# First-weight blocks of a joint matrix product: split by the loader or ahead of the store

## The chip, the cores and the metric

One core of one Trainium2 chip. The metric is the time of one execution on the device in microseconds (us), as the median of several runs. Engines are named as in the profile: PE (TensorE matmuls), PEld (its weight loads), DVE (VectorE), ACT (ScalarE), POOL (GpSimd), SP (SyncE, which mostly issues DMAs). "SPq" is SP's own queue of instructions.

## The reference

Attention within chunks of 64 positions, followed by a mixer of rank 32 along the sequence and a two-layer network with relu:

```python
B, H, S, D = 8, 8, 576, 64          # chunk = 64, so 9 chunks per head
scores = scale * q_c @ k_c.T        # in each chunk of 64
attn = exp(scores - max(scores));  attn = attn / sum(attn)
x = (attn @ v_c)                    # put back to [8, 576, 512]
xt = x.transpose(0, 2, 1)
h = xt @ U @ V                      # U [576, 32], V [32, 576]
u = x + h.transpose(0, 2, 1)
ch = maximum(u @ w_ch1, 0.0) @ w_ch2    # 512 -> 2048 -> 512
return u + ch
```

All inputs and the output are float32. On the chip a float32 operand of the big products is split into a high part rounded to fp32r and a low part (value minus high part), and a product of two operands is made of three: high by high, high by low, low by high.

## The kernel before, in words

The eight batches form four pairs `pr`. A pair has nine tiles of 128 positions by 512 channels (in three groups of three). In time the kernel has these parts, by the profiled run:

- **0 to 150 us, lead.** The weights are brought in and split into high and low parts (the areas `area[f]`, sixteen of them, one for each 128 of the 2048 hidden channels, with both weight matrices of that block), and pair 0 goes through attention. A planner sets the order.
- **150 to about 416 us, blocks.** Seven groups of three tiles go through the two layers block by block: `hidden` (L1070), relu and split (L1078 on ACT, L1083 on DVE), `project_out` (L1098). Between the blocks stand the "visits", which do the attention of a later pair (scores L894, softmax L907 to L921, values L949, the turn of the exponentials through HBM as `exs` and `eT`, split of x L974 on ACT and L978 on DVE or POOL, the product with U L991/L992) and the "mixes", which add V's part and put the mixed rows to HBM (`xd`, `xb`, `ud`, `xs`, `uf`).
- **416 us to the end, `joint`.** The remaining eight groups go two at a time through four rounds (`JOINT`), each of 4 chunks. Here the first layer is not computed block by block but with Strassen's scheme in Winograd's form: seven products of sums of weights with sums of activations instead of eight. In a chunk there are fourteen such product steps (A1 to A7 and B1 to B7, named in `STEPS`; six matmuls each, L1495) and twelve output steps (Ga0 to Gb5, L1471). After certain steps ACT copies a bank (`snap`, L1426), DVE adds to a bank (L1429, L1441), and ACT and DVE make the relu and its split (L1437, L1438). The sums of activations for the next round are made by POOL (`csum`, L1365 to L1371) and split by ACT (L1391) and DVE (L1392).

Each product step needs one block of (sums of) first weights, 256 by 256 numbers. These are made once, in `combos(i)` for i = 0 to 7: POOL builds the sums (L1285 to L1290), `parts` splits them on ACT (L1296) and on the side chosen by `queues` (L1297) and puts them to HBM as `wc[i]`, `plain_parts` puts the three unsummed blocks there from the areas, where high and low part lie already (L1309, L1310). They come back as a stream of 224 blocks (4 rounds x 4 chunks x 14 steps) of high and low part together, 256 KB each: `issue(n)` loads block n to `window(n)`, one of `LOADS = 11` places; the load of block n + 11 is issued right after product n. To make room for these places and for the sums of activations, `gather(i)` copies the second weights of every odd area into the even one before it, HBM not being involved.

What sets the order: after the lead, everything but the blocks hangs in an agenda by ticks (`at(tick, name, run)`); three or four ticks are a block, one tick is one step of `joint`. A table `TUNE["shift"]` adds to the tick of each named piece (as `"wpart 0": 4`), and `TUNE["queues"]` says on which queue its DMA is issued (S, P, A for SP, POOL, ACT) or, for the subtractions of splits (`xl`, `clo`, `wlo`), whether POOL ("P") or DVE makes them. Instructions of one engine run in the order in which they are written; a DMA whose data or place is not ready holds up everything behind it on the queue that issues it. `dma(kind, ...)` (L217) issues nearly all DMAs, so that line 217 stands for all kinds, and the tile names tell them apart.

Of the kernel before, what the change touches and what calls it, by code (L numbers as in the profile page):

```python
# [1669 lines left out]
```

## Time and profile before

| | |
|---|---|
| three runs | 1020.01, 1016.02, 1019.69 us; median 1019.69 us |
| the profiled execution | 1021.43 us, of which the span from first to last instruction is 1019.6 us |
| mean granted clock of PE | 0.956 of full speed |
| PE, DVE, ACT, POOL busy | 90%, 58%, 29%, 21% of the span |
| mean busy share of the 16 DMA engines | high (0.8 to 0.97) from 225 to 750 us, 0.48 after that |

How to read it: PE is the engine with most work, so the time is PE's work at full clock plus what PE stands idle plus what a lower granted clock adds. A view by stretches of time gives for each stretch each engine's busy time, the granted clock (PEclk, 1.0 is full speed) and the busy share of the DMA engines; a view of waits gives what ended each of PE's idle times; the chain of waits follows the end of the run back to what released each step.

### The profile page before, as it was taken

Reading aid. Unit: us, or ns where it says so; the run is one execution under the profiler, and the core shown is the slowest. Engines: PE = TensorE matmul, PEld = TensorE weight load, DVE = VectorE, ACT = ScalarE, POOL = GpSimd, SP = SyncE. Lnnn points to the kernel's source line nnn. Section 1 sums busy time; section 2 is a strip of 40 time slices with the busy share of each in tenths; the row PEclk is TensorE's granted clock in tenths of the full one; section 3 lists DMA queues with packets and bytes.
Section 4 is the critical chain, followed back from the end, with each engine's and each line's share of the span. In section 5 each row is a group of like instructions: output and inputs, shape, how many; then the busy total and the mean of one; then the engine's idle time right before and its main releaser. Section 6 shows DMA issues by size and latency. Waiting matters only on the chain.

```text
span 1019.6 us, 17395 instructions
## 1 busy us (share of the span) xinstructions
PE 917.1 (90%) x6404; PEld 796.1 (78%) x6404; DVE 592.5 (58%) x1134; ACT 300.8 (29%) x600; POOL 213.0 (21%) x318
## 2 busy tenths in 40 slices
PE   6899999988868868989589899897989999999998
PEld 5579988876757757969477797886978998799987
DVE  4899975674645544855567745555553545644333
ACT  5576731222212112412031521222331322222211
POOL 4200002376824111402022601102320011200000
PEclk9999999999879978989699999988999999999999
DMA  9975756678789998999699887938745667364311
GB/s 181 225 265 146 198 125 147 145 217 207 207 252 290 262 251 249 285 253 236 179 232 225 263 255 204 251 105 226 225 145 175 207 193 231 108 212 145 124 52 63
DMA packets 329796, 202.94 MB, mean 199 GB/s; under 512 B 202480, under 2 KB 276240, under 8 KB 329712
## 3 DMA queue, kind: packets, MB, share of 16 engines
q1 hardware_dynamic: 215904, 168.25, 56.9%
q10 hardware_dynamic: 106320, 15.37, 9.1%
q0 software_dynamic: 7488, 18.21, 6.4%
q8 instruction: 51, 0.84, 0.3%
q14 instruction: 33, 0.27, 0.1%
HBM read 145.93 MB, written 65.80 MB: 208 GB/s over the span
## 4 chain that ended last, share of the span: by engine, by line
PE 49%; DMA 10%; DVE 5%; SPq 4%; issue 1%; ACT 1%; ACTq 0%; DVEq 0%
PE o L1471 23%; SPq L217 4%; PE o L1098 3%; DMA eT<-exs 3%; DMA w<-wc 3%; PE h L1070 3%; PE x_0B L1495 2%; PE x_1A L1495 2%; PE x_0A L1495 1%; PE x_2A L1495 1%; PE x_1B L1495 1%; DVE w L1392 1%; PE x_3A L1495 1%; PE x_3B L1495 1%; PE as L949 1%
## 5 line engine op out<-in xcount | busy, mean ns | idle before, releaser
L1070 PE MATMUL h<-uth,w 128*128 128x384 f32 x512 | 144.9, 349 | 7.9 <-DVE x L961 7.9
L1479 DVE TENSOR_TENSOR xr<-o,xr 128x512 f32<-128x512 f32 x96 | 65.5, 687 | 112.2 <-PE o L1471 102.2
L1098 PE MATMUL o<-w,hh 128*128 128x512 f32 x384 | 124.2, 405 | 2.2 <-ACT hh L1078 2.2
L217 POOL DMA_DIRECT2D vn<-in_v_dram x104 | 63.9, 625 | 221.0 <-PE as L894 136.8
L1070 PEld LDWEIGHTS h<-uth,w 128*128 128x128 f32 x512 | 98.0, 196 | 11.5 <-issue 9.3
L1070 PE MATMUL h<-utl,w 128*128 128x384 f32 x256 | 89.3, 349 | 0.0
L1098 PEld LDWEIGHTS o<-w,hh 128*128 128x128 f32 x384 | 72.6, 193 | 15.7 <-ACT hh L1078 3.5
L1098 PE MATMUL o<-w,hl 128*128 128x512 f32 x192 | 78.2, 407 | 1.9 <-DVE hl L1083 1.9
L1078 ACT ACTIVATE hh<-h 128x384 fp32r<-128x384 f32 x64 | 31.0, 488 | 124.8 <-PE h L1070 120.6
L1083 DVE SCALAR_TENSOR_TENSOR hl<-h,hh 128x384 fp32r<-128x384 f32 x64 | 34.9, 548 | 38.1 <-ACT hh L1078 37.9
L949 PE MATMUL as<-vn,eT 64*64 64x64 f32 x864 | 26.4, 252 | 32.2 <-DMA eT<-exs 21.9
L914 ACT ACTIVATE ex<-ex 128x512 f32<-128x512 f32 x27 | 17.1, 632 | 127.8 <-DVE ex L908 105.7
L1070 PEld LDWEIGHTS h<-utl,w 128*128 128x128 f32 x256 | 50.2, 196 | 2.6 <-issue 0.2
L949 PEld LDWEIGHTS as<-vn,eT 64*64 64x64 f32 x864 | 22.1, 161 | 35.8 <-issue 23.6
L1098 PEld LDWEIGHTS o<-w,hl 128*128 128x128 f32 x192 | 36.9, 192 | 13.9 <-DVE hl L1083 5.5
L217 POOL DMA_DIRECT2D xb<-xd x22 | 12.2, 556 | 135.3 <-DMA xd<-x 30.8
L907 DVE TENSOR_REDUCE mx<-as 128x4 f32<-128x256 f32 x54 | 22.5, 416 | 27.8 <-PE as L949 26.2
L874 DVE STREAM_TRANSPOSE qn<-qn 128x512 f32<-128x512 f32 x27 | 19.0, 704 | 31.1 <-DMA qn<-qblocks 28.8
L1471 PE MATMUL o<-w,hh_3B 128*128 128x512 f32 x96 | 32.5, 422 | 0.0
L1471 PE MATMUL o<-w,hh_0A 128*128 128x512 f32 x96 | 31.8, 414 | 0.0
L1471 PE MATMUL o<-w,hh_1A 128*128 128x512 f32 x96 | 31.5, 410 | 0.0
L1471 PE MATMUL o<-w,hh_1B 128*128 128x512 f32 x96 | 31.5, 410 | 0.0
(338 smaller groups left out, 2092.9 us busy)
## 6 DMA issues: line engine op xcount, KB each, us to landing
w<-wc SPq DMA_DIRECT2D x220, 256.0 KB, 3.7
wraw<-in_moe_w_ch_dram SPq DMA_DIRECT2D x32, 512.0 KB, 5.8
xs<-xb SPq DMA_DIRECT2D x112, 64.0 KB, 3.2
uf<-xs SPq DMA_DIRECT2D x27, 256.0 KB, 4.6
vn<-in_v_dram POOLq DMA_DIRECT2D x104, 64.0 KB, 4.2
kblocks<-in_k_dram ACTq DMA_DIRECT2D x23, 288.0 KB, 6.0
qblocks<-in_q_dram ACTq DMA_DIRECT2D x22, 288.0 KB, 6.1
exs<-ex SPq DMA_DIRECT2D x96, 64.0 KB, 3.2
```

The lines of the kernel that those rows point to most:

```text
L217: {"S": nc.sync, "P": nc.gpsimd, "A": nc.scalar}[way].dma_start(dst, src)
L874: nc.vector.transpose(z, z)
L907: nc.vector.reduce_max(mx[:, e], self.sc[e].rearrange("p (h k) -> p h k", k=C), axis=AX.X)
L914: nc.scalar.activation(exf, exf, AF.Exp, scale=SCALE)
L949: nc.tensor.matmul(ps[e][cs, (HP + hp) * C : (HP + hp + 1) * C], lhsT=self.eT[rows, hp, 2 * c : 2 * c + 2, :].rearrange("p a i -> p (a i)" ...
L1070: nc.tensor.matmul(ps[:, :GN], lhsT=w[:, z, cc], rhs=u[:, cc, :], start=(n == 0), stop=(n == 3 * NCC - 1))
L1078: nc.scalar.activation(hh, ps[:, :GN], AF.Relu)
L1083: nc.vector.scalar_tensor_tensor(hl, ps[:, :GN], 0.0, hh, op0=ALU.max, op1=ALU.subtract)
L1098: nc.tensor.matmul(acc[j], lhsT=h[:, js], rhs=w2[f][:, z], start=(first and i == 0), stop=(final and i == 2),)
L1471: nc.tensor.matmul(acc[j], lhsT=u[:, q, js], rhs=w2[f][:, p], start=(z == "A" and e == 0 and n == 0), stop=(z == "B" and e == 1 and n == 2),)
L1479: nc.vector.tensor_add(xs[j], acc[j], xs[j])
L1495: nc.tensor.matmul(ps, lhsT=w[:, wz ^ low_first, cc], rhs=u[uz][:, cc], start=(k in (1, 2, 5) and cc == 0 and m == 0), stop=(cc == 1 and m ...
```

## The change

The stream holds single float32 blocks instead of high and low parts. `combos(i)` makes the sums as before on POOL, but in four regions of the two spare tiles, and `put()` stores all seven blocks of an i, the plain ones among them (POOL's first two additions make high plus low, which is the plain float32 weight), in four DMAs of kind `wput`. `parts`, `plain_parts` and `gather` are gone, and with the last the moved second weights: `window(n)` is now a pair of half-size places, one in the first weights' part of an even area and one in that of the odd one, and a load brings 128 KB into the low place. New is `split_w(n)`: ACT rounds the block from the low place into the high place (L1321 of the new kernel), then POOL (or DVE for four of the 224, by `queues`) subtracts in place so that the low part stays (L1322). It stands in the program behind product n - 5 (`AHEAD = 5`), the first five at ticks of their own (`wsplit`). The first loads are due five ticks earlier (+9 for +14). Both tables of `TUNE` are replaced as a whole; among other things the fetches of `xb` go from POOL's queue to SP's, and most exceptions for single transfers are gone. Lines behind the tables stand 16 to 18 lower than before.

Counted in the two programs: SP issues 868 DMAs instead of 830; ACT has 859 instructions instead of 652, POOL 489 instead of 318, DVE 1126 instead of 1134; PE has 5238 in both.

```diff
-        "wsum 4": 2.5, "wsum 5": -2.75, "wsum 6": -6, "wsum 7": 5
...
+        "wsplit 1": -4, "wsplit 2": -1.75, "wsplit 3": -2, "wsplit 4": 0.25, "wsum 0": 4.0,
...
-        "clo 3.0.5": "S", "clo 3.1.3": "S", "clo 3.2.4": "P", "fetch": "P", "fetch 1_1": "S",
...
+    QUEUES = {"vn": "P", "perm": "A", "wlo": "P", **TUNE.get("queues", {})}
...
     LOADS = 11
+    AHEAD = 5
...
         def sums():
             done.add(("sum", i))
-            assert i < 2 or ("parts", i - 2) in done
-            wc[i] = dram.tile([7, P, 2, KC], F32, name=f"wc_{i}")
-            st["b"] = rooms()
...
+            assert not i or ("put", i - 1) in done
+            one, two, r1, r2 = st["b"] = [region(k) for k in range(4)]
...
-        def parts():
-            done.add(("parts", i))
-            for t, k in zip(st["b"], (3, 5)):
-                h, b = t[:, DM : 2 * DM], t[:, i % 2 * 2 * DM :][:, 0:DM]
-                nc.scalar.copy(h, b.bitcast(F32))
-                side("wlo", i).tensor_sub(b, b.bitcast(F32), h)
-                nc.sync.dma_start(
...
+        def put():
+            done.add(("put", i))
+            if not i % 2:
+                wc[i // 2] = dram.tile([P, len(ORDER), KC], F32, name=f"wc_{i // 2}")
+            to = wc[i // 2]
+            one, two, r1, r2 = st["b"]
+            for src, ks in ((one, (1, 2)), (two[:, KC:], (3,)), (r1, (5, 4)), (r2, (6, 7))):
...
-    def plain_parts(i):
...
-        nc.sync.dma_start(wc[i][0:2].rearrange("k p z x -> p z k x"), one)
-        nc.sync.dma_start(wc[i][2], two[:, :, 1])
...
-    def gather(i):
...
-        dma("gather", even[:, 0 : 2 * DM].bitcast(F32), odd[:, 2 * DM :].bitcast(F32))
...
     def window(n):
         k = n % LOADS
         if k < 7:
-            return whole[2 * k + 1][:, 6 * KC : 8 * KC]
-        return whole[NF - 1][:, (k - 7) * 2 * KC : (k - 6) * 2 * KC]
+            return [area[2 * k + z][:, 3 * KC :] for z in range(2)]
+        k -= 7
+        a = area[2 * 7 + k // 2][:, (k % 2) * 2 * KC : (k % 2 + 1) * 2 * KC]
+        return [a[:, 0:KC], a[:, KC:]]
...
-        dma("w", window(n).bitcast(F32), wc[i][KEPT[k]].rearrange("p z x -> p (z x)"), n)
+        dma("w", window(n)[1].bitcast(F32), wc[c][:, o], n)
+
+    def split_w(n):
+        if n >= BLOCKS_OF * len(JOINT):
+            return
+        assert ("issue", n) in done
+        done.add(("wsplit", n))
+        h, l = window(n)
+        nc.scalar.copy(h, l.bitcast(F32))
+        side("wlo", n).tensor_sub(l, l.bitcast(F32), h)
...
                     issue(n + LOADS)
+                    split_w(n + AHEAD)
...
-        at(f"wpart {i}", FIRST + 6 * i + 5, parts)
-        at(f"wplain {i}", 182 + 5 * i, lambda i=i: plain_parts(i))
-        at(f"gather {i}", 192 + 8 * i + 4, lambda i=i: gather(i))
+        at(f"wput {i}", FIRST + 6 * i + 5, parts)
...
-        at(f"first {n}", 192 + 8 * n + 14, lambda n=n: issue(n))
+        at(f"first {n}", 192 + 8 * n + 9, lambda n=n: issue(n))
+        if n < AHEAD:
+            at(f"wsplit {n}", 192 + 8 * n + 16, lambda n=n: split_w(n))
```

How the instructions of three engines stand now. A row names the line, the operation, the tile written, the tile read, and its shape; the number at the end of a name is the tile's own; "x4" is four like it in a row.

SP in the part from 300 to 415 us, before; `w<-w` of 1024 columns is a gather, `wc<-w` a plain part, `w<-wc` the first loaded block, `exs` and `eT` the turn of the exponentials, `qn` and `kn` the loads of a visit:

```order
L217 DMA w_614<-w_951 128x1024
L217 DMA qn_2_3503<-qblocks_2435 128x4x128
L217 DMA kn_2_3504<-kblocks_2436 128x4x128
L217 DMA qn_3_3580<-qblocks_2435 128x4x128
L217 DMA kn_3_3581<-kblocks_2436 128x4x128
L217 DMA exs_0_3593<-ex_0_3486 32x4x128 x4
L217 DMA xd_8_3605<-x_8_3493 128x512
L217 DMA eT_0_3607<-exs_0_3593 128x4x32 x4
L217 DMA w_951<-wc_2379 128x512
L1309 DMA wc_2746<-w_1396 256x2x256
L1310 DMA wc_2746<-w_1454 256x1x256
L217 DMA eT_1_3623<-exs_1_3616 128x4x32 x4
```

The same engine and place now, where `xb<-xd` is a fetch:

```order
L201 DMA qn_2_3480<-qblocks_2439 128x4x128
L201 DMA kn_2_3481<-kblocks_2440 128x4x128
L201 DMA w_951<-wc_2393 128x256
L201 DMA exs_0_3526<-ex_0_3454 32x4x128 x4
L201 DMA exs_1_3540<-ex_1_3464 32x4x128 x4
L201 DMA xb_6_3545<-xd_6_3197 128x512
L201 DMA qn_3_3572<-qblocks_2439 128x4x128
L201 DMA kn_3_3573<-kblocks_2440 128x4x128
L201 DMA xb_4_3581<-xd_4_2857 128x512
L201 DMA xb_5_3592<-xd_5_2864 128x512
L201 DMA eT_1_3611<-exs_1_3540 128x4x32 x4
L201 DMA w_1082<-wc_2393 128x256
```

Gathers and plain parts are gone from the row, the loads of blocks are half as wide, and the fetches stand in it.

ACT in chunk 1 of the last round, before; L1426 is a copy of a bank, L1437 a relu:

```order
L1426 COPY s_3_1A<-x_1A 128x384
L1426 COPY s_3_1A<-c_1A 128x384
L1426 COPY u_3_1A<-x_1A 128x384
L1437 ACTIVATE hh_1A<-y_1A 128x384
L1437 ACTIVATE hh_1A<-c_1A 128x384
L1426 COPY s_3_1B<-x_1B 128x384
L1426 COPY u_3_1A<-x_1A 128x384
```

The same engine and place now; L1408 is the copy, L1419 the relu, L1321 the rounding of a loaded block:

```order
L1408 COPY s_3_1A<-x_1A 128x384
L1321 CAST w_1021<-w_1082 128x256
L1408 COPY s_3_1A<-c_1A 128x384
L1321 CAST w_1128<-w_1160 128x256
L1321 CAST w_1219<-w_1259 128x256
L1408 COPY u_3_1A<-x_1A 128x384
L1419 ACTIVATE hh_1A<-y_1A 128x384
L1321 CAST w_1306<-w_1353 128x256
L1321 CAST w_1396<-w_1454 128x256
L1419 ACTIVATE hh_1A<-c_1A 128x384
L1408 COPY s_3_1B<-x_1B 128x384
L1321 CAST w_1500<-w_1550 128x256
```

One rounding per product step has come between the copies and relus.

POOL in the first round, before; `vn` are loads of v for a visit, `xb` fetches:

```order
L217 DMA vn_4_4452<-in_v_dram 64x4x64 x4
L217 DMA vn_5_4489<-in_v_dram 64x4x64 x4
L217 DMA xb_2_4746<-xd_2_4232 128x512
L217 DMA xb_1_4775<-xd_1_4049 128x512
L217 DMA xb_3_4835<-xd_3_4257 128x512
L217 DMA vn_7_4939<-in_v_dram 64x4x64 x4
L217 DMA vn_6_4979<-in_v_dram 64x4x64 x4
L217 DMA vn_8_5186<-in_v_dram 64x4x64 x4
```

The same engine and place now; L1322 is the subtraction that leaves the low part:

```order
L1322 TENSOR_TENSOR w_1454<-w_1454,w_1396 128x256
L201 DMA ud_1_4943<-xb_1_4819 128x512
L1322 TENSOR_TENSOR w_1550<-w_1550,w_1500 128x256
L1322 TENSOR_TENSOR w_1607<-w_1607 128x256 x2
L1322 TENSOR_TENSOR w_1649<-w_1649 128x256
L201 DMA vn_7_5024<-in_v_dram 64x4x64 x4
L1322 TENSOR_TENSOR w_1649<-w_1649 128x256
L201 DMA vn_8_5227<-in_v_dram 64x4x64 x4
L201 DMA vn_1_5243<-in_v_dram 64x4x64 x4
L1322 TENSOR_TENSOR w_1082<-w_1082,w_1021 128x256
```

Subtractions stand on POOL's queue in front of and behind the loads of v.

## Rows read from the trace of the kernel before

**Rows 1.** The page's line of busy time, share of the span and instructions.

```profile
PE 917.1 (90%) x6404; PEld 796.1 (78%) x6404; DVE 592.5 (58%) x1134; ACT 300.8 (29%) x600; POOL 213.0 (21%) x318
```

**Rows 2.** Stretches: length, busy PE, PEld, DVE, ACT, POOL, PEclk, DMA share, GB/s.

```profile
225.00:300.00 75.00, 56.13 (x432) 47.96 (x433) 44.22 (x79) 14.72 (x27) 48.60 (x60) 0.85 0.84 219
300.00:415.00 115.00, 96.44 (x759) 83.67 (x758) 61.29 (x128) 24.05 (x51) 28.42 (x42) 0.92 0.97 266
415.00:750.00 335.00, 293.27 (x2076) 255.00 (x2076) 202.22 (x413) 89.13 (x204) 69.94 (x106) 0.93 0.81 220
750.00:1019.60 269.60, 263.52 (x1323) 234.85 (x1322) 115.14 (x200) 66.34 (x151) 18.35 (x27) 0.99 0.48 153
```

**Rows 3.** PE's waits, 225 to 300 us: total us, times, longest.

```profile
PE as L949 <- DVE hl L1083: 7.3, 1, 7.3
```

**Rows 4.** PE's waits, 300 to 415 us.

```profile
PE y L991 <- ACT xh L974: 9.3, 1, 9.3
```

**Rows 5.** PE's waits, 415 to 750 us.

```profile
PE as L949 <- DMA eT<-exs: 16.8, 13, 3.5
```

**Rows 6.** The chain of waits, 340 to 396 us: start, duration, what.

```profile
362.82 4.07 DMA xs<-xb
```

**Rows 7.** The chain of waits, 474 to 500 us.

```profile
477.39 7.96 DMA w<-wc
```

**Rows 8.** DMA, 300 to 415 us: totals; issues with count, KB, median us to landing.

```profile
DMA packets 51035, 30.62 MB, mean 266 GB/s; under 512 B 28958, under 2 KB 45345, under 8 KB 51025
...
wc<-w SPq DMA_DIRECT2D x8, 512.0 KB, 5.4
w<-w SPq DMA_DIRECT2D x8, 512.0 KB, 4.8
wc<-w SPq DMA_DIRECT2D x8, 256.0 KB, 5.4
w<-wc SPq DMA_DIRECT2D x8, 256.0 KB, 3.7
```

**Rows 9.** DMA, 415 to 750 us, the same view.

```profile
DMA packets 116776, 73.79 MB, mean 220 GB/s; under 512 B 69187, under 2 KB 92739, under 8 KB 116748
...
w<-wc SPq DMA_DIRECT2D x113, 256.0 KB, 4.3
...
eT<-exs SPq DMA_DIRECT2D x48, 64.0 KB, 3.7
```

**Rows 10.** Groups by line and form: count, busy us, mean ns, idle before, releaser.

```profile
L1391 ACT CAST w<-us 128x256 fp32r<-128x256 f32 x48 | 17.4, 404 | 7.3 <-POOL us L1369 2.8 <-POOL us L1371 2.3 <-POOL us L1365 1.9
L1371 POOL TENSOR_TENSOR us<-uf,uf 128x256 f32<-128x256 f32 x12 | 9.7, 820 | 6.7 <-DVE w L1392 6.7
L217 POOL DMA_DIRECT2D vn<-in_v_dram x104 | 63.9, 625 | 221.0 <-PE as L894 136.8 <-DVE qn L874 20.0 <-PE as L949 19.4
L1297 DVE TENSOR_TENSOR wch<-wch 128x512 fp32r<-128x512 f32 x8 | 9.9, 1237 | 14.4 <-ACT wch L1296 14.4
L978 DVE TENSOR_TENSOR xl<-x,xh 128x512 fp32r<-128x512 f32 x23 | 15.5, 683 | 14.9 <-ACT xh L974 11.5 <-DMA xs<-xb 2.1 <-DMA exs<-ex 1.1
```

**Rows 11.** The waits of SP's own queue, 225 to 300 us.

```profile
SPq L1298 <- DVE wcl L1297: 8.4, 1, 8.4
```

**Rows 12.** Timeline, 927 to 931 us: start, duration, engine, line, instruction.

```profile
928.70 1.20 PE L1495 MATMUL c_1B<-w,w 128*128 128x384 f32 x6
928.95 0.48 ACT L1426 COPY u_1A<-x_1A 128x384 f32<-128x384 f32 x1 [0.35 <-PE x_1A L1495]
...
929.74 1.20 PE L1495 MATMUL x_1A<-w,w 128*128 128x384 f32 x6
```

**Rows 13.** POOL's waits, 415 to 750 us.

```profile
POOL us L1365 <- DMA uf<-xs: 30.2, 4, 18.5
...
POOL vn L217 <- DVE qn L874: 20.0, 1, 20.0
POOL vn L217 <- PE as L949: 19.4, 2, 18.8
```

More of the change, by code (lines that the diff above doesn't have):

```diff
@@ L1266, in combos, with region @@
         st = {}
[L1268 to L1269 removed]
+        def region(k):
+            if not turned_w:
                 for z in "hl":
[L1271 removed]
+                    turned_w[z] = work.tile([P, NCC, GN], F32, tag="ut" + z, name="wc" + z, bufs=2).rearrange(
                         "p c t -> p (c t)"
                     )
[L1274 to L1275 removed]
+            z, k = divmod((4 * i + k) % 6, 3)
+            return turned_w["hl"[z]][:, k * DM : (k + 1) * DM]
         def sums():
             done.add(("sum", i))
[L1279 to L1282 removed]
+            assert not i or ("put", i - 1) in done
+            one, two, r1, r2 = st["b"] = [region(k) for k in range(4)]
             for b, f in ((one, 2 * i), (two, 2 * i + 1)):
@@ L1303, in combos @@
-        return sums, parts
-    def plain_parts(i):
-        assert ("gather", i) not in done
-        done.add(("plain", i))
-        one, two = (area[f].bitcast(F32).rearrange("p (z k x) -> p z k x", z=2, k=2) for f in (2 * i, 2 * i + 1))
-        nc.sync.dma_start(wc[i][0:2].rearrange("k p z x -> p z k x"), one)
-        nc.sync.dma_start(wc[i][2], two[:, :, 1])
-    stream = [
-        (2 * c + "AB".index(z[0]), int(z[1])) for _ in JOINT for c in range(CHUNKS) for z in STEPS if z[0] != "G"
-    ]
@@ L1316, in gather @@
-    def gather(i):
-        assert ("plain", i) in done and ("sum", i) in done and ("hidden", 1, 0, 2 * i) in done
-        done.add(("gather", i))
-        even, odd = (whole[f] for f in (2 * i, 2 * i + 1))
-        dma("gather", even[:, 0 : 2 * DM].bitcast(F32), odd[:, 2 * DM :].bitcast(F32))
-        moved[2 * i + 1] = even[:, 0 : 2 * DM].rearrange("p (s x) -> p s x", s=2)
-    moved = {}
+            nc.gpsimd.tensor_sub(r1[:, a], two[:, a], one[:, a])
+            nc.gpsimd.tensor_sub(r2[:, z], two[:, z], two[:, a])
@@ new lines, in sums @@
+            nc.gpsimd.tensor_sub(r2[:, a], two[:, z], r1[:, a])
+            nc.gpsimd.tensor_sub(r1[:, z], one[:, z], r2[:, a])
+        def put():
[5 more added lines that the diff above has]
+            for src, ks in ((one, (1, 2)), (two[:, KC:], (3,)), (r1, (5, 4)), (r2, (6, 7))):
+                at = [ORDER.index("AB"[i % 2] + str(k)) for k in ks]
+                dma(
+                    "wput",
+                    to[:, at[0] : at[-1] + 1 : max(1, at[-1] - at[0])],
+                    src.rearrange("p (k x) -> p k x", x=KC),
+                    i,
+                )
@@ L1325, in window @@
+        return sums, put
+    ORDER = [z for z in STEPS if z[0] != "G"]
+    BLOCKS_OF = len(ORDER) * CHUNKS
     def window(n):
@@ L1384, in split @@
             done.add(("split", self.s, j, k))
-            assert ("gather", i) in done and ("out", 1, 0, 2 * i + 1) in done
+            assert free(2 * i + 1)
             assert not self.s or ("last", self.s - 1, k) in done
@@ L1487, in joint @@
                     loads[0] += 1
-                    w = window(n).rearrange("p (z c f) -> p z c f", z=2, c=2)
-                    low_first = KEPT[k] > 2 and not (2 * c + "AB".index(z)) % 2
+                    w = [v.rearrange("p (c f) -> p c f", c=2) for v in window(n)]
                     u = combo(k)
@@ L1496, in joint @@
                                 ps,
-                                lhsT=w[:, wz ^ low_first, cc],
+                                lhsT=w[wz][:, cc],
                                 rhs=u[uz][:, cc],
@@ L1502, in joint @@
                             )
-                    assert ("issue", n) in done and all(("split", s, i, k) in done for i in range(GT))
+                    assert ("wsplit", n) in done and all(("split", s, i, k) in done for i in range(GT))
                     done.add(("product", n))
@@ L1632 @@
             pend = (pr, g, f, hs)
-    w2.update({f: moved[f] for f in range(1, NF, 2)})
     for n in range(7, LOADS):
```

27 lines of the change are left out of this document (7 added, 20 removed), and 253 rows, old and new, of the table TUNE.

## The prediction

> **What bounds the kernel now.** I read the page's busy line first: PE works 917.1 us of a span of 1019.6 [rows 1], so about 102 us are to be had at most without touching its work, plus what a lower clock adds. The second view, the stretches, tells where. For each I add PE's idle time and the part of its busy time that the clock below 1.0 costs, (1 - PEclk) times busy [rows 2]: 225 to 300 us loses 18.9 + 8.4 = 27.3; 300 to 415 loses 18.6 + 7.7 = 26.3; 415 to 750 loses 41.7 + 20.5 = 62.2; 750 to the end only 6.1 + 2.6 = 8.7. The third view, PE's waits, tells on what: between 225 and 300 us the longest ends with DVE's split of the relu [rows 3]; between 300 and 415 with ACT's rounding of a visit's x [rows 4], whose data come through HBM; between 415 and 750 the waits for the turned exponentials `eT` lead with 16.8 us in 13 waits [rows 5]. No row names a block of first weights as what PE waited for, so the stream itself is early enough. The last view, the chain, shows how it acts all the same: it passes through transfers that took long when the DMA engines were full, a 64 KB `xs` of 4.07 us [rows 6], and once through a block load of 7.96 us [rows 7], against which the median load of the stretch lands in 4.3 us [rows 9]; from that landing the chain goes on with SP's own next issues, so that what was queued behind it on SP started late. In the stretches from 225 to 750 us the DMA engines are 0.81 to 0.97 busy, behind 750 us 0.48 [rows 2]. So fewer bytes and fewer issues can buy time only before 750 us, and there they act on waits that other transfers end.
>
> **The parts of the change.** The sum is made on the profiled run, 1021.4 us, which is its span and 1.8 us around it; the median of the runs is 1.7 lower.
>
> *1. Gathers and plain parts gone (300 to 415 us).* Removed from this stretch are 8 gathers and 8 plain parts of 512 KB and 8 plain parts of 256 KB, 8 x 1280 KB = 10.5 MB, and half of 8 loads of 256 KB, 1.0 MB: 11.5 of 30.62 MB, or 38% [rows 8]. 24 issues leave SP's queue. DMA is the fullest resource here (0.97), and what PE loses is mostly late data, so I let the loss shrink in proportion: 38% of 26.3 = **-10.0**. Bounds: 0, if the waits are latency and not load, and -26.3, if all of it goes.
>
> *2. Loads of half the size (415 to 750 us).* 113 loads lose 128 KB each, 14.8 of 73.79 MB, 20% [rows 9]. In proportion: 20% of 62.2 = **-12.4**. Bounds: 0, and -41.7, the whole idle time. Behind 750 us as many loads shrink too, but PE is idle for 6.1 us there: nothing.
>
> *3. Split of the sums gone (225 to 300 us).* Sixteen subtractions leave DVE, the eight of one half alone 9.9 us [rows 10], and as many roundings leave ACT. SP waited 8.4 us for one of these subtractions before it could store its result [rows 11]; it now waits for POOL's sums alone, which are unchanged. The stores are as large as before within a fifth (8 x 896 KB for 16 x 512 KB). Of the 7.3 us that PE waits for DVE's relu split [rows 3], behind which those subtractions stood in part, I take about half: **-4**. Bounds: 0 and -18.9, the idle time of the stretch.
>
> *4. Rounding and splitting each block.* No such instruction is in the trace, but ACT rounds the same shape in 404 ns and POOL subtracts it in about 820 ns [rows 10]: 224 x 0.404 = 90 us more on ACT, 220 x 0.82 = 180 us more on POOL. Both have the room on average: ACT goes from 301 to about 380 us (ten of them back from part 3), POOL from 213 to about 393. What counts is where they stand. In a joint round product steps follow each other by 1.04 us (928.70 to 929.74). ACT's copy of a bank starts 928.95 and takes 0.48, so the bank is free at 929.43, and PE's next product in that bank begins at 929.74: a margin of 0.31 us [rows 12]. A rounding put right before such a copy begins earlier than the copy could (ACT was idle for 0.35 us there), so that it is covered in most places; uncovered it would cost 0.404 - 0.31 = 0.09 us for each of 128 copies, 12 us. At the three ends of rounds, where ACT also rounds the next sums in a row, two roundings more stand between the copies after B6 and B7: 3 x 2 x 0.404 = **+2.4**. On POOL a subtraction has a cover of four to five products, since its block is needed five products later: 5 x 1.04 - 0.40 - 0.82 = 4.0 us. Bounds: 0 and 12 + 2.4 = +14.4.
>
> *5. The order.* PE's own order is nearly the same; visits move by a step or so. The 22 fetches of `xb` go from POOL's queue to SP's, behind which `exs`, `eT` and the block loads wait if a fetch waits for its data. What a new order gives or takes is not in any row; I bound it by the longest single waits of the two stretches, 7.3 and 9.3 us [rows 3, 4], as about 8 us either way, and take **0**, since the transfers that were moved to SP replace 24 that left it.
>
> Sum: -10.0 - 12.4 - 4 + 2.4 = -24.0, so 1021.4 - 24.0 = 997.4 on the profiled run; 1.7 less for the median: **about 995.5 us**, rounded to 995.
>
> **The rivals.**
>
> *A. The relief does not reach PE: about 1020.* The stream is halved but the waits stay. For it: a 64 KB `eT` lands in 3.7 us, a 256 KB block in 4.3 [rows 9], so that size matters little once a transfer is alone, and PE's largest sum of waits is on `eT` [rows 5]. Against it: the `xs` of 4.07 and the load of 7.96 us [rows 6, 7] are long for their size, which is load. Parts 1 to 3 at nothing and +2.4 for part 4 make 1023.8 on the profile; a little relief in part 1 alone makes it 1020 on the median. The Trainium skill, "DMA: Bandwidth & Descriptors", section "Anatomy of one DMA — SWDGE (gpsimd) path", speaks for this rival: it fits a transfer as some 2.0 us fixed plus bytes over 436e3, by which an estimate for a load is 2.6 us at 256 KB and 2.3 at 128 KB. By it part 2 would be worth 0.3 us on a load that PE does not wait for, nothing in the sum. The page speaks of transfers that GpSimd issues and these are SP's; the median landing of 4.3 us is 1.7 us longer than the estimate, which is what the trace says of queueing.
>
> *B. POOL's queue becomes the bound (slower): about 1037.* POOL works in order. Loads of v wait in its queue until PE has freed their place, and sums for the next round wait for their data: between 415 and 750 us 30.2, 20.0 and 19.4 us in seven waits [rows 13]. If subtractions stand behind these, the weights of the next products come late, and PE stops in the middle of a round. Each wait has 4.0 us of cover: 69.6 - 7 x 4.0 = 41.6 us, which on 997.4 makes 1039.0, or 1037 on the median. It makes the kernel slower from about 24 us on. For it: subtractions do stand right behind the loads `vn_7`, `vn_8` and `vn_1` in the new order, and one wait lasts 18.8 us. Against it: those waits belong to loads issued early; the new table moves most of the loads of v, and what waited with nothing behind it can be put where it waits for nothing.
>
> *C. The clock comes back as well: about 974.* PE's clock is at 0.92 and 0.93 in the stretches in which it pauses and 0.99 where it doesn't [rows 2]. If the pauses get short enough for the full clock, 7.7 + 20.5 = 28.2 us of clock loss go from 300 to 750 us, and idle time goes in proportion, 38% of 18.6 and 20% of 41.7, 15.4. With -4 and +2.4 the sum is -45.2: 976.2, or 974 on the median. Against it: visits, which cause the pauses by their chain through HBM, all stay.
>
> *D. POOL and DVE slow each other: about 1010.* DVE's subtraction of two tiles took 1237 ns while POOL made the sums of the weights, and the same shape 683 ns in the visits [rows 10]. With 220 more subtractions on POOL the same 0.55 us may come on DVE's two-input splits. On the path are those at the three ends of rounds, three tiles times three late sums: 27 x 0.55 = 14.9 us, 1012.3 or 1010 on the median. A rule of the Trainium skill speaks for this: "SBUF — State Buffer", section "Who interferes with whom", has one port pair shared by the two engines under an exclusive lock, and a DVE instruction with two SBUF inputs contends with a GpSimd one that reads SBUF. The two rows agree with it, but they don't show which of the two engines was first.
>
> **How the numbers follow.** Forecast 995: 0.43. Rival B 0.18, as the only new serial queue; C 0.15; A 0.14; D 0.10. A measurement of this kernel can tell about 0.5%, 5 us, from no change. Faster by more: the forecast, C, nearly all of D and a little of A, 0.43 + 0.15 + 0.09 + 0.02 = 0.69. Within: most of A, the edges of B and D, 0.10 + 0.01 + 0.01 = 0.12. Slower: B and the rest of A, 0.17 + 0.02 = 0.19. The range goes from somewhat below C, 968, to 1030: this takes in A, D and the half of B in which only some of its seven waits reach PE, and leaves out about 0.09 above and as much below, where all bounds of parts 1 to 3 are met.
>
> **What would show it.** Part 1: in the stretch from 300 to 415 us, which should end about 10 us earlier, the DMA share falls from 0.97 and the wait on `xh` shrinks. Part 2: the loads land sooner than 4.3 us and the sum of `eT` waits falls below 16.8 us. Part 3: SP no longer waits there for DVE, and the wait for L1083 is about half. Part 4: PE's waits on ACT's copies in the last 270 us stay within some 3 us of 6.1 us idle; ACT is near 380 and POOL near 393 us busy. B would show as PE waiting at the product steps for POOL's L1322; D as DVE's splits of sums rising from their present means; C as a clock of 0.97 or more from 415 to 750 us. The forecast is wrong if the stretches before 750 us keep their lengths, or if the stretch behind it, now full, gets longer.

## The result, and the profile after

The changed kernel takes 987.5 us in the median of three runs (986.96 to 987.66), against 1019.69 before: a ratio of 0.9694, 95% interval 0.9659 to 0.9728, or 32 us less. 995 had been forecast, so the sign and the order of size are right, and the gain was larger than the 24.7 us forecast.

The busy line and the stretches of the changed kernel (columns as in [rows 2], the last stretch being shorter by what was won):

```profile
PE 907.8 (92%) x6404; PEld 788.2 (80%) x6404; DVE 590.7 (60%) x1126; ACT 360.0 (37%) x808; POOL 346.7 (35%) x489
```

```profile
225.00:300.00 75.00, 59.03 (x456) 49.53 (x455) 38.38 (x81) 12.21 (x24) 40.45 (x51) 0.90 0.89 225
300.00:415.00 115.00, 103.99 (x828) 90.90 (x826) 69.38 (x148) 33.40 (x82) 40.33 (x59) 0.99 0.76 190
415.00:750.00 335.00, 304.60 (x2164) 265.07 (x2165) 209.46 (x404) 123.86 (x315) 143.03 (x195) 0.95 0.68 177
750.00:985.90 235.90, 229.63 (x1127) 204.67 (x1125) 107.25 (x181) 86.18 (x227) 79.60 (x104) 0.99 0.32 96
```

PE is idle for 11.0 us between 300 and 415 us where it was 18.6, its granted clock there is 0.99 for 0.92, and the DMA engines are 0.76 busy for 0.97 [rows 2]. From 415 to 750 us idle time falls from 41.7 to 30.4 us, DMA from 0.81 to 0.68. The last stretch keeps its 6 us. DMA from 300 to 415 us and from 415 to 750 us:

```profile
DMA packets 46905, 21.90 MB, mean 190 GB/s; under 512 B 30751, under 2 KB 42184, under 8 KB 46894
...
w<-wc SPq DMA_DIRECT2D x18, 128.0 KB, 3.9
```

```profile
DMA packets 118879, 59.30 MB, mean 177 GB/s; under 512 B 70052, under 2 KB 108565, under 8 KB 118847
...
w<-wc SPq DMA_DIRECT2D x116, 128.0 KB, 3.3
eT<-exs SPq DMA_DIRECT2D x56, 64.0 KB, 3.2
```

Against [rows 8, 9] a block lands in 3.3 us instead of 4.3 in the second stretch, and `eT` in 3.2 instead of 3.7; in the first a block of half the size lands no sooner (3.9 us for 3.7). PE's waits of 225 to 300 us and of 415 to 750 us (total, times, longest), and SP's own of 225 to 300 us:

```profile
PE y L975 <- ACT xh L958: 8.2, 1, 8.2
PE as L933 <- DMA eT<-exs: 3.1, 5, 1.3
```

```profile
PE as L933 <- DMA eT<-exs: 10.9, 13, 4.0
PE x_0B L1476 <- ACT u_0B L1408: 5.9, 2, 4.3
PE x_3B L1476 <- ACT u_3B L1408: 3.7, 2, 2.4
PE x_2A L1476 <- ACT u_2A L1408: 3.0, 1, 3.0
PE as L878 <- DVE kn L858: 2.9, 1, 2.9
PE x_1B L1476 <- ACT u_1B L1408: 2.2, 2, 1.1
PE c_3B L1476 <- POOL w L1322: 1.4, 1, 1.4
```

```profile
SPq L201 <- POOL wch L1273: 2.5, 1, 2.5
```

The wait for the relu split [rows 3] is gone; SP's wait of 8.4 us for a subtraction of the sums [rows 11] has become one of 2.5 us for POOL's sums and two shorter ones. The wait of 9.3 us for `xh` [rows 4], before the eleventh of the visits' products with U, is gone; before the ninth, of an earlier visit, there is now one of 8.2 us. In the joint rounds PE now waits longest for ACT's copies of banks (L1408), and once for a split block (L1322). Waits for copies are not new, however: from the start of round 1 on they are 14.8 us in the kernel before and 18.3 now, while those for `eT` fall from 16.8 to 10.9. Their largest row before, from 417 us on:

```profile
PE x_3B L1495 <- ACT u_3B L1426: 8.4, 3, 3.8
```

Fixed stretches of time mix different work, so for the rest I cut each run at places of the program: the start of the first matmul of every eighth block of hidden units, and of each joint round, from the trace; round 4 goes to the end of PE's last matmul. Ahead of the joint rounds stand four groups of three tiles (not seven, as the description of the kernel has it), of sixteen such blocks each, so that blocks 32 to 63 are the last two groups. Us in each part, in one profiled execution of each kernel:

| kernel | start of block 32 | blocks 32-39 | 40-47 | 48-55 | 56-63 | round 1 | round 2 | round 3 | round 4 |
|---|---|---|---|---|---|---|---|---|---|
| before | 200.8 | 57.2 | 56.7 | 56.3 | 45.8 | 179.7 | 161.1 | 132.3 | 126.3 |
| changed | 202.5 | 43.2 | 59.9 | 43.9 | 43.0 | 177.7 | 153.4 | 133.0 | 126.3 |
| b_noparts | 200.6 | 57.1 | 57.2 | 45.5 | 41.8 | 181.0 | 166.6 | 130.5 | 126.3 |
| b_half | 199.6 | 57.5 | 56.4 | 55.9 | 42.6 | 172.9 | 154.5 | 130.2 | 126.3 |
| b_nosub | 200.1 | 47.6 | 60.0 | 53.8 | 43.9 | 178.8 | 164.6 | 132.3 | 126.3 |
| b_all3 | 201.9 | 48.3 | 60.0 | 45.5 | 44.7 | 172.5 | 154.4 | 130.0 | 126.3 |
| a_nosplit | 201.5 | 48.0 | 56.5 | 44.5 | 44.5 | 179.0 | 144.4 | 128.4 | 126.3 |
| a_oldorder | 204.0 | 48.6 | 55.3 | 45.4 | 42.6 | 180.4 | 170.9 | 142.5 | 126.3 |
| o_nosplit | 198.7 | 48.7 | 55.8 | 45.5 | 42.8 | 169.6 | 153.8 | 132.6 | 126.3 |
| o_dve | 200.1 | 48.4 | 55.4 | 45.4 | 43.5 | 176.9 | 156.8 | 136.1 | 126.5 |
| a_dve | 200.5 | 46.9 | 56.2 | 44.5 | 44.4 | 176.0 | 155.2 | 131.6 | 126.6 |
| a_cast2 | 201.4 | 43.6 | 59.3 | 42.8 | 46.5 | 182.0 | 161.3 | 136.2 | 128.1 |
| a_late5 | 201.3 | 46.4 | 58.4 | 43.9 | 44.4 | 177.9 | 155.1 | 129.6 | 126.3 |
| a_late10 | 201.0 | 44.5 | 59.4 | 43.8 | 44.0 | 176.8 | 150.3 | 129.2 | 126.3 |

The changed kernel's 33 us are thus 14.0 in blocks 32 to 39, 12.4 in 48 to 55, 2.8 in 56 to 63 and 9.0 in rounds 1 to 3, less 3.2 in blocks 40 to 47 and 1.7 ahead of block 32.

### The profile page after: what moved, and what is told of

The parts are those of the page before. It is cut to its first block, busy times and chain, and to the rows that moved or that the text cites. A ratio compares the mean times of both kernels' runs of the same rounds, so it can differ in the third digit from the quotient of the medians.

```text
span 985.9 us, 17952 instructions
## 1 busy us (share of the span) xinstructions
PE 907.8 (92%) x6404; PEld 788.2 (80%) x6404; DVE 590.7 (60%) x1126; ACT 360.0 (37%) x808; POOL 346.7 (35%) x489
## 4 chain that ended last, share of the span: by engine, by line
PE 59%; DMA 15%; DVE 9%; SPq 5%; ACT 5%; issue 4%; POOL 3%; ACTq 0%; DVEq 0%; POOLq 0%
PE o L1453 24%; PE o L1082 8%; PE h L1054 8%; SPq L201 4%; DMA kblocks<-in_k_dram 4%; DMA qblocks<-in_q_dram 2%; DMA qkv<-in_q_dram 1%; DMA eT<-exs 1%; DMA wraw<-in_moe_w_ch_dram 1%; PE x_2A L1476 1%; DMA xb<-xd 1%; PE x_1A L1476 1%; PE x_2B L1476 1%; DMA w<-wc 1%; PE x_0A L1476 1%
## 5 line engine op out<-in xcount | busy, mean ns | idle before, releaser
L1322 POOL TENSOR_TENSOR w<-w,w 128x256 fp32r<-128x256 f32 x142 | 107.4, 768 | 197.6 <-ACT w L1321 193.3
L1054 PE MATMUL h<-uth,w 128*128 128x384 f32 x512 | 141.5, 342 | 2.1 <-DVE x L945 2.1
L1321 ACT CAST w<-w 128x256 fp32r<-128x256 f32 x224 | 86.9, 408 | 35.7 <-DMA w<-wc 22.4
L1054 PEld LDWEIGHTS h<-uth,w 128*128 128x128 f32 x512 | 95.1, 191 | 5.6 <-issue 3.6
L1322 POOL TENSOR_TENSOR w<-w 128x256 fp32r<-128x256 f32 x78 | 60.2, 785 | 94.2 <-ACT w L1321 94.1
L1054 PE MATMUL h<-utl,w 128*128 128x384 f32 x256 | 87.3, 341 | 0.0
L1067 DVE SCALAR_TENSOR_TENSOR hl<-h,hh 128x384 fp32r<-128x384 f32 x64 | 35.0, 547 | 46.0 <-ACT hh L1062 45.8
L898 ACT ACTIVATE ex<-ex 128x512 f32<-128x512 f32 x27 | 17.1, 632 | 108.8 <-DVE ex L892 62.2
L1054 PEld LDWEIGHTS h<-utl,w 128*128 128x128 f32 x256 | 48.7, 190 | 2.7 <-issue 0.2
L933 PE MATMUL as<-vn,eT 64*64 64x64 f32 x864 | 22.8, 235 | 14.2 <-DMA eT<-exs 14.0
L1374 DVE TENSOR_TENSOR w<-us,w 128x256 fp32r<-128x256 f32 x48 | 29.4, 632 | 7.1 <-ACT w L1373 7.1
L933 PEld LDWEIGHTS as<-vn,eT 64*64 64x64 f32 x864 | 19.3, 146 | 17.1 <-issue 15.4
```

The source lines that it names most:

```text
L933: nc.tensor.matmul(ps[e][cs, (HP + hp) * C : (HP + hp + 1) * C], lhsT=self.eT[rows, hp, 2 * c : 2 * c + 2, :].rearrange("p a i -> p (a i)" ...
L1054: nc.tensor.matmul(ps[:, :GN], lhsT=w[:, z, cc], rhs=u[:, cc, :], start=(n == 0), stop=(n == 3 * NCC - 1))
L1067: nc.vector.scalar_tensor_tensor(hl, ps[:, :GN], 0.0, hh, op0=ALU.max, op1=ALU.subtract)
L1321: nc.scalar.copy(h, l.bitcast(F32))
L1322: side("wlo", n).tensor_sub(l, l.bitcast(F32), h)
L1374: side("clo", f"{self.s}.{j}.{k}").tensor_sub(l, x, h)
```

## The experiments

Two questions: does each of the three reliefs bring what the trace shows at its place, and what do the splits and the new order cost or give? Each ratio is to the kernel before, run on the same chip, with its 95% interval; us gained are the ratio's distance from 1 times 1019.7.

**The three reliefs alone, in the kernel before.** `b_noparts`:

```diff
-        nc.sync.dma_start(wc[i][0:2].rearrange("k p z x -> p z k x"), one)
-        nc.sync.dma_start(wc[i][2], two[:, :, 1])
+        if i == 0:
+            nc.sync.dma_start(wc[i][0:2].rearrange("k p z x -> p z k x"), one)
+            nc.sync.dma_start(wc[i][2], two[:, :, 1])
...
-        dma("gather", even[:, 0 : 2 * DM].bitcast(F32), odd[:, 2 * DM :].bitcast(F32))
...
-        dma("w", window(n).bitcast(F32), wc[i][KEPT[k]].rearrange("p z x -> p (z x)"), n)
+        dma("w", window(n).bitcast(F32), wc[0 if KEPT[k] < 3 else i][KEPT[k]].rearrange("p z x -> p (z x)"), n)
```

> The kernel before without its 8 gathers and without 14 of its 16 plain parts (the block loads read the plain parts of i = 0 instead, so the output is not the reference's). Theory P (bytes and issues of the removed transfers held PE up between 200 and 417 us): 8 to 16 us faster than before, all of it before the first joint round. Theory O (the new order is what shortened that part, the bytes were hidden): within 4 us of before.

Measured: 1007.95 us, 0.9877 (0.9812 to 0.9941), 12.5 us. The interval allows 6 to 19 us. The table puts it where theory P did: blocks 48 to 55 take 45.5 us for 56.3, blocks 56 to 63 41.8 for 45.8; the joint rounds gain nothing, and in this trace they are 5 us longer. From 300 to 415 us PE's wait for `xh` [rows 4] is gone from the list, whose head is now the first row here, the clock is 0.98, and the DMA engines are 0.84 busy:

```profile
PE y L992 <- DVE xl L978: 4.2, 4, 1.8
```

```profile
300.00:415.00 115.00, 106.63 (x836) 93.67 (x836) 72.54 (x154) 30.29 (x67) 34.63 (x51) 0.98 0.84 219
```

`b_half`:

```diff
-        dma("w", window(n).bitcast(F32), wc[i][KEPT[k]].rearrange("p z x -> p (z x)"), n)
+        dma("w", window(n)[:, 0:KC].bitcast(F32), wc[i][KEPT[k]][:, 0], n)
```

> The kernel before, whose block loads bring only the first half of a block (128 KB; the other half of each place is stale, so the output is not the reference's). Theory P: 6 to 13 us faster, all of it between 417 and 760 us. Theory A (the size of a load does not reach PE): within 4 us of before.

Measured: 999.79 us, 0.9814 (0.9774 to 0.9854), some 19 us, more than theory P's 6 to 13. The size of a load does reach PE, and rival A falls. The table has 3.2 us of it already in blocks 56 to 63, where the first loads stand, 13.4 in rounds 1 and 2 and 2.1 in round 3. From 415 to 750 us idle time is 29.1 us and the clock 0.95:

```profile
415.00:750.00 335.00, 305.91 (x2152) 267.65 (x2152) 205.11 (x419) 91.30 (x207) 69.28 (x104) 0.95 0.70 183
```

```profile
w<-wc SPq DMA_DIRECT2D x117, 128.0 KB, 3.2
exs<-ex SPq DMA_DIRECT2D x52, 64.0 KB, 2.4
eT<-exs SPq DMA_DIRECT2D x52, 64.0 KB, 3.2
```

Not only the blocks land sooner (3.2 us for 4.3) but `eT` as well (3.2 for 3.7), whose size is the same [rows 9]. PE's waits for `eT` shrink only from 16.8 to 14.9 us, though; those for ACT's copies fall from 14.8 to 11.4, and the following wait of before, from 415 to 750 us, is gone:

```profile
PE as L894 <- DVE kn L874: 5.4, 1, 5.4
```

`b_nosub`:

```diff
-                side("wlo", i).tensor_sub(b, b.bitcast(F32), h)
```

> The kernel before without the 16 subtractions of the split of the sums (L1297), so the low parts are wrong. Theory P: 4 to 11 us faster, between 200 and 315 us, because DVE's queue and SP's wait for it go. Theory O: within 3 us of before.

Measured: 1013.39 us, 0.9932 (0.9899 to 0.9965), some 7 us. Blocks 32 to 39 lose 9.6 us, and blocks 40 to 47 give 3.3 back, where PE now waits 8.6 us for POOL's split of a visit's x (0.8 us before). PE's waits from 200 to 300 us:

```profile
PE y L992 <- POOL xl L978: 8.6, 1, 8.6
...
PE as L949 <- DVE hl L1083: 2.4, 1, 2.4
PE h L1070 <- DVE x L961: 1.4, 2, 0.8
```

In the kernel before the last of these rows is, in the same window:

```profile
PE h L1070 <- DVE x L961: 6.6, 2, 5.6
```

So 5.2 us of it went, and the wait for L1083 is down from 7.3 us [rows 3] to 2.4.

`b_all3` has the edits of all three.

> The three edits together: gathers and 14 plain parts left out, loads of 128 KB, no subtractions of the sums; no rounding per block, and the order of before. Theory P: the parts add up, 20 to 35 us faster than before, which leaves the new order about nothing. Theory O: under 12 us faster, and the rest of the 32 us is the order's.

Measured: 986.65 us, 0.9657 (0.9606 to 0.9709), 35 us; the three alone add to 12.5 + 19 + 7 = 38.5. In the table each of its parts is about that of the kernel which changes it, but for blocks 56 to 63, which two of them shorten. Theory P holds, and the reliefs without the splits bring all of the changed kernel's gain. That leaves the splits and the order, which must about cancel.

**The splits and the order.** `a_nosplit`, in the changed kernel:

```diff
         h, l = window(n)
-        nc.scalar.copy(h, l.bitcast(F32))
-        side("wlo", n).tensor_sub(l, l.bitcast(F32), h)
```

> The changed kernel without the rounding on ScalarE and the subtraction on GpSimd of each loaded block (the high places keep old data, so the output is not the reference's). Theory H (the splits are hidden, as the forecast has it: 2.4 us at the ends of rounds): 983 to 987 us, with the stages of the joint rounds within 2 us each. Theory C (they cost what the halved stream did not give in the first joint chunk, which got 6 us longer): 975 to 981 us, and the first joint chunk falls from 51 us to about 45.

Measured: 978.59 us, 0.9587 (0.9515 to 0.9659). Against the changed kernel's 0.9694 that is 1.1%, 10.9 us for 224 splits. The size is loose: the intervals touch at 0.9659, the four runs spread from 967.4 to 982.7 us, the ratios of the medians (0.9684 and 0.9621) differ by 6.4 us and the traces by 10.0. Neither theory had the place right. The first chunk of round 1 takes 45.0 us before, 51.3 in the changed kernel and 52.5 without any split: it is the new order that makes it longer. It holds as many attention matmuls in all three, but in the new order PE waits in it for a visit's `kn` (4.3 us without splits, 2.9 in the changed kernel, nothing before) and 1.5 us at its first product. The splits cost 9 us in round 2 and 4.6 in round 3, and in round 4 nothing: 126.3 us with and without.

`a_oldorder` is the changed kernel with the old two tables; what belongs to the new stream keeps the new numbers (a shortened diff):

```diff
-        "cget 0.0.1": 2.25, "cget 0.1.0": -12, "cget 0.1.1": 0.25, "cget 0.1.2": 3,
+        "cget 0.0.0": 2, "cget 0.0.1": 1.25, "cget 0.0.2": -1, "cget 0.1.0": 3, "cget 0.1.1": -3,
...
-        "clo 0.2.5": "S", "clo 2.1.2": "S", "clo 2.2.4": "S", "clo 2.2.7": "S", "fetch 2_0": "S",
+        "clo 3.0.5": "S", "clo 3.1.3": "S", "clo 3.2.4": "P", "fetch": "P", "fetch 1_1": "S",
...
```

> The changed kernel with the table of ticks and queues of the kernel before, but for the pieces that belong to the new stream (its sums, stores, first loads and splits keep the new numbers). Theory N (the order is worth nothing, the three reliefs carry all): 980 to 992 us. Theory O (the new order is what makes room for the splits on ACT's and POOL's queues): 995 to 1015 us, with PE waiting for splits behind GpSimd's loads of v.

Measured: 1020.02 us, 1.0023 (0.9985 to 1.0062). In the old order the change brings nothing at all; theory O holds, and the time is above the 995 to 1015 us that it had given. Blocks 32 to 63 are no longer than in `b_all3`, but rounds 1 to 3 lose it all again. PE's waits from 400 us on, where L1197 is the subtraction that leaves the low part and L1283 ACT's copy:

```profile
PE x_3B L1351 <- ACT u_3B L1283: 11.4, 3, 4.4
PE as L808 <- DMA eT<-exs: 10.1, 10, 2.4
...
PE x_2A L1351 <- POOL w L1197: 4.6, 1, 4.6
PE x_2B L1351 <- POOL w L1197: 3.8, 1, 3.8
PE x_3A L1351 <- ACT u_3A L1283: 3.8, 1, 3.8
...
PE x_1A L1351 <- POOL w L1197: 3.5, 1, 3.5
```

And the timeline of the 4.6 us, with POOL, ACT's roundings (L1196) and PE's product:

```profile
820.18 0.41 ACT L1196 CAST w<-w 128x256 fp32r<-128x256 f32 x1
...
821.70 0.41 ACT L1196 CAST w<-w 128x256 fp32r<-128x256 f32 x1
...
824.60 0.55 POOL L76 DMA_DIRECT2D xb<-xd  x1 [8.86 <-DMA ud<-xb]
825.17 1.41 POOL L1197 TENSOR_TENSOR w<-w,w 128x256 fp32r<-128x256 f32 x2
...
825.96 1.49 PE L1351 MATMUL x_2A<-w,w 128*128 128x384 f32 x4 [4.62 <-POOL w L1197]
```

POOL stood for 8.86 us at the issue of a fetch that waited for the store `ud` of an earlier tile. The roundings for its next subtractions were done at 820.6 and 822.1, so that the first of them stood ready for some 4 us of these. As soon as the fetch is issued the subtractions run, and PE goes on. The other two long waits for a subtraction also come right behind a fetch, one held for 7.34 us at 449.9 us and this one:

```profile
672.90 0.54 POOL L76 DMA_DIRECT2D xb<-xd  x1 [7.26 <-DMA ud<-xb]
```

Together the three are 11.9 of the 13.4 us that PE waits there for a block's subtraction. The changed kernel issues the fetches on SP; its corresponding wait is 1.4 us, once, behind a sum.

`o_nosplit` is `a_oldorder` with the edit of `a_nosplit`; `o_dve` is `a_oldorder`, and `a_dve` the changed kernel, with

```diff
-        side("wlo", n).tensor_sub(l, l.bitcast(F32), h)
+        nc.vector.tensor_sub(l, l.bitcast(F32), h)
```

> The changed kernel with the old table of ticks and queues and without rounding and subtraction of the blocks (the high places keep old data, so the output is not the reference's). Theory S (in the old order it is the splits that cost the 33 us): 978 to 990 us, as the kernel before with the three reliefs alone. Theory F (something else of the new code costs it in the old order, the stores or the first loads): over 1005 us.

Measured: 979.88 us, 0.9633 (0.9593 to 0.9672). Without splits the old order is as good as the new one (0.9587, whose interval holds 0.9633). So what costs the 40 us in `a_oldorder` is the splits and nothing else of the new code. Its largest row of waits for a copy, from 391 us on, for comparison with the next kernel:

```profile
PE x_3B L1349 <- ACT u_3B L1281: 8.1, 3, 3.8
```

> The changed kernel with the old table of ticks and queues and all 224 subtractions on DVE. Theory B (GpSimd's in-order queue, in which subtractions stand behind loads of v and fetches, holds the blocks up): 985 to 1003 us, and PE no longer waits for a block's subtraction. Theory A (the roundings on ScalarE delay its copies): 1010 to 1030 us, no gain against the 1020 us with GpSimd.

Measured: 993.86 us, 0.9779 (0.9727 to 0.9831). Moving only the subtractions from POOL to DVE gives back 25 of the 40 us, and no wait of PE names a block's subtraction any more. The other 15 stay, as waits on ACT's copies, which are 27.2 us in the joint rounds against 12.0 in `o_nosplit`:

```profile
PE x_3B L1351 <- ACT u_3B L1283: 11.3, 3, 4.7
...
PE x_1B L1351 <- ACT u_1B L1283: 5.2, 2, 2.6
```

Theory B holds for the larger part. That the rest is theory A's roundings is argued and not shown: in `a_oldorder`, with the same roundings and the subtractions on POOL, the copies cost 19.9 us.

> The changed kernel with all 224 subtractions of the blocks on DVE instead of 220 on GpSimd. Theory H (GpSimd hides them): DVE gets some 115 us more work in its queue, 990 to 1005 us, joint rounds longer. Theory B (GpSimd's in-order queue holds blocks up): 978 to 986 us, faster than the changed kernel.

Measured: 986.66 us, 0.9699 (0.9648 to 0.9751), the same as the changed kernel. Both theories are wrong: DVE has room for 224 subtractions in these rounds, and in the new order POOL's queue no longer holds up what matters. Which engine subtracts is indifferent there for the time as a whole, but not for the waits: those for ACT's copies grow from 18.3 to 25.6 us, those for `eT` shrink from 10.9 to 5.3.

> The changed kernel with the rounding of each block made twice (224 more instructions of 0.41 us on ScalarE, the result the same). Theory H (a rounding stands in ACT's idle time, margin 0.31 us before a copy of a bank is late): 988 to 995 us. Theory C (each rounding delays ACT's copies, which PE waits for): 1000 to 1030 us, the last joint round longer than its 126.4 us.

```diff
         nc.scalar.copy(h, l.bitcast(F32))
+        nc.scalar.copy(h, l.bitcast(F32))
```

Measured: 1000.43 us, 0.9847 (0.9799 to 0.9896), 15.6 us more than the changed kernel by the ratios and 13 by the medians, about where theory C begins; its trace is of the slowest of the four runs, 1005.9 us. Round 4, which has only the products, grows by 1.8 us for 56 roundings (23 us of ACT's time): there they are nearly hidden. Rounds 1 to 3 grow by 4.3, 7.9 and 3.2 us: where ACT also serves visits and the next round's sums, they are not.

PE's waits from the start of round 1 on, added up by what ended them, in us (- where no block is split; the last two kernels follow below):

| kernel | for ACT's copies | for `eT` | for a block's subtraction |
|---|---|---|---|
| before | 14.8 | 16.8 | - |
| changed | 18.3 | 10.9 | 1.4 |
| a_nosplit | 10.0 | 8.2 | - |
| a_oldorder | 19.9 | 10.1 | 13.4 |
| o_nosplit | 12.0 | 13.1 | - |
| o_dve | 27.2 | 9.3 | 0 |
| a_dve | 25.6 | 5.3 | 0 |
| a_cast2 | 24.9 | 6.7 | 0.8 |
| a_late5 | 12.0 | 9.8 | 1.2 |
| a_late10 | 11.6 | 11.3 | 1.8 |

**Splits moved away from the copies.** One place where such waits arise is the end of a round. Timeline of the changed kernel at the end of round 3, where L1351 makes sums for the next round on POOL, L1373 rounds them on ACT, and L1322 is a block's subtraction:

```profile
836.18 0.92 POOL L1351 TENSOR_TENSOR us<-uf,us 128x256 f32<-128x256 f32 x1
...
837.06 0.91 POOL L1322 TENSOR_TENSOR w<-w,w 128x256 fp32r<-128x256 f32 x1
...
837.30 2.67 DVE L1374 TENSOR_TENSOR w<-us,w 128x256 fp32r<-128x256 f32 x3
...
837.93 0.90 POOL L1351 TENSOR_TENSOR us<-uf,us 128x256 f32<-128x256 f32 x1
838.80 0.90 POOL L1322 TENSOR_TENSOR w<-w,w 128x256 fp32r<-128x256 f32 x1
838.87 0.40 ACT L1373 CAST w<-us 128x256 fp32r<-128x256 f32 x1 [0.94 <-POOL us L1351]
839.18 0.40 ACT L1321 CAST w<-w 128x256 fp32r<-128x256 f32 x1
839.48 0.47 ACT L1408 COPY u_3B<-x_3B 128x384 f32<-128x384 f32 x1
...
840.01 1.71 PE L1476 MATMUL x_3B<-w,w 128*128 128x384 f32 x6 [2.46 <-ACT u_3B L1408]
```

Sums and subtractions take turns on POOL; each sum comes 0.9 us later for the subtraction between; ACT's roundings of the sums wait for them, and the copy that PE needs stands behind these in ACT's order. PE stops for 2.46 us. That this taking turns makes the stop is not shown, however. At the same product, the last of round 3, PE also stops in the kernel before, which has no block to split, and in `a_dve`, where POOL has no block's subtraction:

```profile
873.34 1.34 PE L1495 MATMUL x_3B<-w,w 128*128 128x384 f32 x6 [2.10 <-ACT u_3B L1426]
```

```profile
840.29 1.32 PE L1476 MATMUL x_3B<-w,w 128*128 128x384 f32 x6 [2.83 <-ACT u_3B L1408]
```

In `a_nosplit` it does not stop there. So in the new order the splits make the stop, but not by their turns on POOL alone. After B4 a chunk has ten output steps without any product. `a_late5` and `a_late10` split the next chunk's first 5 or 10 blocks there (the edit of `a_late10`):

```diff
     loads = [0]
+    todo_w = [AHEAD]
...
+                    if i > STEPS.index("B4") and loads[0] <= todo_w[0] < loads[0] + 10:
+                        split_w(todo_w[0])
+                        todo_w[0] += 1
...
-                    split_w(n + AHEAD)
+                    if n % len(ORDER) + AHEAD < len(ORDER) and todo_w[0] <= n + AHEAD:
+                        split_w(n + AHEAD)
+                        todo_w[0] = n + AHEAD + 1
```

> The changed kernel with the splits of the next chunk's first five blocks moved behind B4, one to each of the output steps Gb0 to Gb3 (instead of behind products B2 to B4). Theory E (splits between the sums of the next round hold ACT's copies up at the ends of rounds): 980 to 985 us, the last chunk of rounds 1 and 2 shorter by 1 to 4 us each. Theory H (the splits are hidden where they are): 986 to 989 us.

Measured: 984.2 us, 0.9659 (0.9619 to 0.9699). The place answers as theory E said: the last chunks of rounds 1 and 2 are 1.6 and 1.0 us shorter, and round 3 takes 129.6 us for 133.0. Round 2 as a whole gets 1.7 us longer, and the whole is not told apart from the changed kernel by these intervals.

> The changed kernel with the splits of the next chunk's first ten blocks made in its ten last output steps and only four during the product steps. Theory E: 977 to 984 us, since the product steps, where ACT's copies are waited for, lose ten of fourteen roundings. Theory H: 986 to 989 us. Slower, 990 to 1000 us, if the blocks split early stand in front of DVE's and ACT's relu at the chunk's start.

Measured: 979.75 us, 0.9619 (0.9586 to 0.9652), the fastest complete kernel here: its interval lies below the changed kernel's (0.9659 to 0.9728), and it stands where `a_nosplit` (0.9587, to 0.9659) stands within the intervals. Rounds 1 to 3 take 7.8 us less than in the changed kernel, and the stop at the last product of round 3 is 0.68 us.

## Why the prediction was right, and what was sized wrongly

**What bounds it.** The reading that PE loses time before 750 us to transfers that are late because the DMA engines are full, and that no wait names a block load, was right. `b_half` shows it best: loads that PE never waits for were halved, and 19 us went. The last stretch gave nothing, as said.

**Part 1** was put at -10.0 and measured at -12.5 (`b_noparts`, with 14 of the 16 plain parts gone), which its interval does not tell from the forecast. The trace goes beyond a share of bytes of 38%: from 300 to 415 us the loss falls from 26.3 to 10.5 us, since the 9.3 us wait went as a whole and the clock came back from 0.92 to 0.98; in the same trace rounds 1 and 2 are 7 us longer.

**Part 2** was put at -12.4 and measured at about -19 (0.9814). Of the reliefs this is the one most undersized, and its interval (15 to 23) leaves the forecast out. In proportion to bytes, 20% of the loss of the stretch would go; 17.8 of its 62.2 us went (29.1 idle and 15.3 for the clock are left), and 3 us more in the last blocks before it, where part 1 had counted the loads as 1.0 of 11.5 MB. The gain is spread over several waits, of which `eT`, the largest, gave only 1.9 us.

**Part 3** was put at -4 and measured at -7 (`b_nosub`, 3.6 to 10.3 by its interval). The wait for L1083 falls by 4.9 of 7.3 us, somewhat more than the half taken; the wait of a block for DVE (L961), of which 5.2 us went too, had not been counted.

**Part 4** was put at +2.4 and measured at +10.9 (`a_nosplit`; 6 to 10 by the medians and the traces). Durations were right (roundings 408 ns, subtractions 768 and 785); ACT and POOL are 360 and 347 us busy, not 380 and 393, POOL among other things because it issues 45 DMAs fewer. The margin before copies was right where only products run: round 4 pays nothing. The step that failed is that a rounding before a copy was taken as covered everywhere but at the ends of rounds. Of the 12.4 us by which rounds 1 to 3 are longer with splits than without, in one trace each, 7.5 lie in the first three chunks of round 2, in which visits run, where the term had nothing: the longest wait for a copy there is 4.27 us, 0.96 in `a_nosplit`. The last chunks of the rounds pay 4.6 us for the 2.4 counted. PE's waits for ACT's copies account for 8.3 us (18.3 against 10.0). That roundings have a share is shown by `a_cast2`, which adds them alone and has 24.9 us of these waits; what the subtractions' share is stays open. The bound of +14.4 holds it.

**Part 5** was put at 0, and that hides the main lesson. Without splits the two orders are worth the same (0.9633 and 0.9587). With splits the new one is worth 33 us (0.9694 against 1.0023). The step that failed said that fetches moved to SP only replace issues that left it. They also leave POOL's queue, where they would have held up subtractions, as the three fetches of `a_oldorder` did.

**The sum.** From the ratios in a row: -35.0 for the three reliefs (`b_all3`; forecast -26.4), -2.4 for the rest of the new code in the old order (`o_nosplit`), -4.7 for the new order without splits (`a_nosplit`; neither of these two is outside its error), +10.9 for the splits in the new order: -31.2, where the sum had -24.0. Reliefs too small by 9, splits too small by 8, and 7 us that no term had. That the first two nearly cancel is luck, and the 7 us are what the forecast missed. (1021.4 - 24.0 - 1.7 is 995.7 and not 995.5, which changes nothing.)

**The rivals.** A fell with `b_half`. **B** was the right mechanism and is real: in the old order it costs 25 of 40 us, and makes the kernel as slow as before. It was named with loads of v and the next round's sums in front of the subtractions; in the trace the long waits stand behind fetches of `xb`. What was said against it, that a new table can put what waits where it waits for nothing, is what happened. C: the clock rose to 0.99 from 300 to 415 us but only to 0.95 from 415 to 750, below the 0.97 set for it. D: DVE's splits of sums do slow beside POOL. Counted over the records of the kernel before, 35 of the L1392 subtractions with less than 0.1 us of POOL arithmetic beside them took 416 ns in the mean, 46 with more 730; in the changed kernel 27 took 431 and 57 took 715. The Trainium skill's rule ("SBUF — State Buffer", section "Who interferes with whom") agrees with these numbers. But they were slowed before as well: the means of their two groups are now 632 and 613 ns for 642 and 524, some 2.5 us more in all, where D counted 14.9 us at 0.55 us each, a price read from tiles twice their size. Taking POOL's subtractions away (`a_dve`) brought no time. What D costs PE was not separated.

**Not tried:** the fetches alone back on POOL in the new order, which would show whether that one entry of the table carries the 25 us, of which PE's direct waits for a block's subtraction are 13.4; and roundings without subtractions in the new order, which would separate the two halves of a split.
